# Pooled attention and top-1 experts in one kernel: another order for the first attention unit and for the expert loop

## The chip, the cores and the metric

The kernel runs on one core of one Trainium2 chip. The metric is device time in microseconds (us), the median of a few executions. TensorE (PE in the profile; PEld is its weight load), VectorE (DVE), ScalarE (ACT), GpSimd (POOL) and SyncE (SP, which here issues nearly all DMAs) run side by side and meet only at semaphores. Each engine takes its own instructions in the order in which they are written.

## The reference

```python
# attention: 8 batches, 8 heads, 576 tokens, 64 per head; keys and values are means over 8 tokens (72 of them)
k_p = k.reshape(B, H, Sp, 8, D).mean(axis=3); v_p = v.reshape(B, H, Sp, 8, D).mean(axis=3)
scores = (1 / sqrt(D)) * q @ k_p.T ; attn = softmax(scores) ; x = attn @ v_p      # -> 4608 rows of 512
# experts: 8, each 512 -> 1024 -> 512, one for each row
expert_idx = argmax(x @ w_gate) ; gate_w = softmax(x @ w_gate)[expert_idx]
y[row] = gate_w * (relu(x[row] @ w1[e]) @ w2[e])          # e = expert_idx[row]
```

All arrays are float32. Products in the experts are made of three float16 products each (high by high, high by low, low by high part), those of the scores in float32.

## The kernel before

**Attention.** The 4608 rows are 36 units of 128 rows. Two units with the same batch are a group; a group's queries are turned by TensorE (`g_qt`, L450, copied out by ACT at L453), and its scores are made in four steps of two heads each: `g_s` (the product, L473), `g_min` (DVE, L483), `g_exp` (ACT, L490). Then for each unit: `u_pt` turns the exponentials (L497) and ACT copies them to float16 (L499), `u_lo` makes the low part (DVE, L505), `u_pv` multiplies by the pooled values (L531), `u_nrm` divides (DVE, L563 to L574) and leaves the row block in a ring of 12 slots, `XR`. Later `route` finds the expert of each row, and POOL scatters the rows into one region for each expert in DRAM (`xs`).

For every batch the keys and values are pooled, three additions each. Batch 0 is pooled on DVE in two parts (`pool_now`, L322 to L324), batch 1 on POOL in five pieces of 128 pooled rows (`pool_short`, L306 to L308), later batches on POOL in whole tensors (`pool`, L313 to L316). `k_pe`/`k_act` turn the pooled keys and copy them into the block-diagonal right side `BD` of the score product (`half(b, s)`); `v_pe`/`v_act`/`v_dve`, `u_pe` and `u_dve` (with `masked`, L423) prepare the pooled values `VB`. Where each of these stands in the unit loop is a list of hooks (`put(unit, position, function)`); the positions of a unit are, in order, "q", "pe", "act", "dve", the product `u_pv`, "pe2", "sp", `u_nrm`, "act2", "dve2".

Group 0 and the first step of group 1 are written out ahead of the unit loop (L728 to L771): 36 dummy products, pooling of the keys, the queries' turns, the turns of the pooled keys one 64-column half at a time (L738, L739), their two copies on ACT (L741), then the four score steps with the value work between them.

**Experts.** A first block of 256 rows of expert 0 is multiplied during the last units. The rest are blocks of up to 256 rows in a loop, 21 passes in this run, with tables (`tabs`) that say for each block its row, its expert's weight set, whether a weight set has to be split (`en`), whether a block has more than 128 rows and which expert is to be loaded (`en3`). Weights arrive as float32 in two staging areas (`ST`: st1/st2 and, once the attention has finished, XR and pall) and are split into float16 high (ACT, L105) and low parts (DVE, L107) by `part` in the first block of an expert, for the next expert. A block is: 96 products `up` (L922 to L924), `relu_hi` (ACT, L981) and `relu_lo` (DVE, L985), `arrive` (DVE, L865: the turned x of the next block), `part`, 48 or 24 products `finish` (L991), `take` (ACT, L1170), `give` (POOL, L1173 to L1175: an indirect DMA to the output).

In a pass t the order on the queues is: SP reads its table entries; ACT and DVE run `split_x` (L853, L854: float16 parts of the x of block t+2, which lies in `xg`); SP issues `load_x(t + 3)` into `xg` (L1129); then the block; then SP issues `trans` (L861, a DMA transpose of what `split_x` made), the four weight loads of expert 2 in pass 0 (`If(t < 1)`, L1231, an `If` that every engine evaluates), and up to four weight loads of 1 MB for each staging area (L91, under the `If` at L1235). Where such an `If` isn't taken, SP waits in the other branch until the semaphores of those loads are where they would have been.

## Time and profile before

| | us |
|---|---|
| median of three runs (lowest to highest) | 660.05 (656.13 to 660.56) |
| the profiled execution, as timed | 661.64 |
| its span, first to last instruction | 659.8 |
| PE busy | 588.9 |
| DVE, ACT, POOL busy | 331.9, 286.0, 282.9 |
| mean granted clock of TensorE over the span | 0.961 |

The profile is of one execution. Its page gives busy times by engine, and its views answer for a stretch: a table of busy time by window, a timeline of one engine's instructions with what ended the idle time before each ("[1.78 <-ACT bd L981]" is 1.78 us of idle, ended by the instruction that wrote bd at L981), a list of waits, and the chain of waits that ended last. Instructions of one kind in a row are merged into one line with a count. The name of a buffer is that of its tile: bd holds the relu parts and the parts of x in the expert loop, kv0 the turned x, qt and kv the second weight set.

### The profile page before, as it was taken

The page shows a single profiled execution, that of the slowest core. Times are in us where ns is not written, and L with a number is a line of the kernel's source. Part 1 is how long each engine was busy: PE and PEld are TensorE (multiplying, and loading weights), DVE is VectorE, ACT ScalarE, POOL GpSimd, SP SyncE. Part 2 cuts the span into 40 slices and gives each one's busy share as a digit, 9 for nine tenths or more (in the row PEclk, how much of TensorE's full clock was granted, in tenths as well). Part 3 has the DMA queues.
Part 4 walks back from the last instruction along what each step waited for, and adds up shares of the span by engine and source line. Part 5 has one row for each costly group of instructions (what it writes and reads, how often), then busy time and mean ns, then how long its engine had stood idle before and what let it go on. Part 6 is the DMA issues. An engine that isn't in the chain of part 4 may idle for free. (4 is left out here: it accounts for less than half of the span.)

```text
span 659.8 us, 16297 instructions
## 1 busy us (share of the span) xinstructions
PE 588.9 (89%) x4634; PEld 429.8 (65%) x4635; DVE 331.9 (50%) x680; ACT 286.0 (43%) x631; POOL 282.9 (43%) x543
## 2 busy tenths in 40 slices
PE   6787897898878958997899799999999999999995
PEld 4676796887767544763576566675776666677663
DVE  5578985798896518202576176222362182221212
ACT  2565776777672126212565166123452181222212
POOL 5896589798695631222044242213132123212213
PEclk9998988998898979999899999999999999999998
DMA  9974778976749574953298387543232233312200
GB/s 257 307 233 124 219 221 243 225 238 184 241 98 312 179 175 141 374 163 81 64 308 303 73 269 235 184 116 100 45 90 66 71 80 83 80 48 64 64 16 29
DMA packets 104394, 105.59 MB, mean 160 GB/s; under 512 B 62502, under 2 KB 72742, under 8 KB 104360
## 3 DMA queue, kind: packets, MB, share of 16 engines
q1 hardware_dynamic: 97720, 85.46, 46.4%
q0 software_dynamic: 6640, 19.71, 8.1%
q8 instruction: 18, 0.29, 0.2%
q14 instruction: 16, 0.13, 0.1%
HBM read 71.77 MB, written 22.06 MB: 142 GB/s over the span
## 5 line engine op out<-in xcount | busy, mean ns | idle before, releaser
L991 PEld LDWEIGHTS <-bd 128*128 128x128 f16 x936 | 91.1, 98 | 114.0 <-ACT bd L981 6.7
L854 DVE TENSOR_TENSOR bd<-vb,bd 128x1024 f16<-128x1024 f32 x21 | 25.7, 1225 | 171.3 <-ACT bd L981 158.4
L1174 POOL TENSOR_TENSOR spacer<-ql,iG 1x1 f32<-1x1 f32 x44 | 21.2, 483 | 206.0 <-ACT ql L1170 205.1
L490 ACT ACTIVATE pall<-ps,nmx 128x72 f32<-128x72 f32 x288 | 68.8, 326 | 29.4 <-DVE nmx L483 28.6
L985 DVE SCALAR_TENSOR_TENSOR bd<-pp,bd 128x512 f16<-128x512 f32 x44 | 30.3, 690 | 75.9 <-ACT bd L981 65.6
L981 ACT ACTIVATE bd<-pp 128x512 f16<-128x512 f32 x44 | 26.2, 598 | 95.8 <-PE pp L924 64.9
L1175 POOL DMA_INDIRECT out_dram<-ql,iG x44 | 49.9, 1133 | 22.5 <-issue 21.9
L991 PE MATMUL po<-w,bd 128*128 128x512 f16 x264 | 58.8, 379 | 0.0
L991 PE MATMUL po<-kv,bd 128*128 128x512 f16 x264 | 58.8, 379 | 0.0
L473 PE MATMUL ps<-bd,qT 128*128 128x144 f32 x256 | 51.0, 329 | 5.6 <-ACT pall L490 2.1
L922 PE MATMUL ps<-kv,w 128*128 128x256 f16 (+1 forms) x176 | 44.5, 266 | 11.2 <-DMA kv<-bd 9.0
L991 PE MATMUL pq<-kv,bd 128*128 128x512 f16 x216 | 49.8, 389 | 3.6 <-ACT bd L981 3.6
L922 PE MATMUL ps<-kv,qt 128*128 128x256 f16 (+1 forms) x176 | 46.4, 268 | 6.2 <-issue 5.3
L531 PE MATMUL po<-vb,ph 128*128 128x146 f16 (+2 forms) x384 | 34.2, 237 | 19.3 <-DVE l L572 8.2
L924 PE MATMUL ps<-kv,qt 128*128 128x256 f16 (+1 forms) x176 | 46.2, 268 | 2.2 <-DVE bd L854 1.5
L853 ACT ACTIVATE bd<-vb 128x1024 f16<-128x1024 f32 x21 | 22.2, 1058 | 57.5 <-DMA kv<-bd 27.6
L923 PE MATMUL ps<-kv,qt 128*128 128x256 f16 (+1 forms) x176 | 46.5, 270 | 0.0
L922 PEld LDWEIGHTS <-w 128*128 128x128 f16 x352 | 34.9, 99 | 16.9 <-issue 9.8
L924 PE MATMUL ps<-kv,w 128*128 128x256 f16 (+1 forms) x176 | 44.6, 267 | 1.3 <-DVE w L107 1.3
L473 PEld LDWEIGHTS ps<-bd,qT 128*128 128x128 f32 x256 | 40.5, 217 | 7.7 <-ACT pall L490 4.8
L991 PE MATMUL pq<-w,bd 128*128 128x512 f16 x192 | 43.2, 379 | 2.0 <-ACT bd L981 1.8
L924 PE MATMUL pp<-kv,qt 128*128 128x256 f16 (+1 forms) x176 | 44.7, 263 | 0.0
(234 smaller groups left out, 1394.7 us busy)
## 6 DMA issues: line engine op xcount, KB each, us to landing
st<-in_moe_w_dram SPq DMA_DIRECT2D x20, 1024.0 KB, 9.7
XR<-in_moe_w_dram SPq DMA_DIRECT2D x9, 1024.0 KB, 7.3
vb<-x_by_expert SPq DMA_DIRECT2D x17, 514.0 KB, 3.8
kv<-in_k_dram SPq DMA_DIRECT2D x7, 1024.0 KB
kv<-in_v_dram SPq DMA_DIRECT2D x7, 1024.0 KB
qt<-in_q_dram SPq DMA_DIRECT2D x6, 1024.0 KB
pall<-in_moe_w_dram SPq DMA_DIRECT2D x3, 1024.0 KB, 9.8
qt<-in_q_dram SPq DMA_DIRECT2D x4, 512.0 KB
```

The lines of the kernel that those rows point to most:

```text
L473: nc.tensor.matmul(ps[:, x * 2 * KP:(x + 1) * 2 * KP], t[:, h, :], BD[b % 3][:, :, h, :], start=True, stop=True)
L490: nc.scalar.activation(p[:, h * KP:(h + 1) * KP], ps[:, x * KP:(x + 1) * KP], AF.Exp, bias=nmx[:, x:x + 1], scale=-1.0)
L531: nc.tensor.matmul(po[:, half, cols], a[:, c * 128:(c + 1) * 128], VB[b % 3][:, y, c, sl, 0:CW], start=st, stop=False, skip_group_check=True)
L853: nc.scalar.activation(h[:, :, 0], x, AF.Copy)
L854: nc.vector.tensor_tensor(h[:, :, 1], x, h[:, :, 0], op=OP.subtract)
L922: nc.tensor.matmul(dst, wh, xT[:, d, 0:n], start=(d == 0), stop=False)
L923: nc.tensor.matmul(dst, wh, xT[:, DC + d, 0:n], start=False, stop=False)
L924: nc.tensor.matmul(dst, wl, xT[:, d, 0:n], start=False, stop=(d == DC - 1))
L981: nc.scalar.activation(hT[0][:, 2 * k:2 * k + 2, :].rearrange("p f t -> p (f t)"), pH[k], AF.Relu)
L985: V.scalar_tensor_tensor(l, pH[k], 0.0, h, op0=OP.max, op1=OP.subtract)
L991: nc.tensor.matmul(y, hT[x][:, f, 128 * j:128 * j + 128], W2[s][z][:, f, :], start=(half == x == z == f == 0), stop=(half == z == 1 and f ...
L1175: st = nc.gpsimd.indirect_dma_start(out=out, out_offset=bass.IndirectOffsetOnAxis(ap=iG[:, j:j + 1], axis=0), in_=ys[j], in_offset=None, b ...
```

## The change

It does the following.

- 80 dummy products instead of 36 at the start, and 26 more (`keep_warm`) at four places of the first unit's steps.
- The pooled keys of batch 0 are written twice side by side by the last addition, so that one turn of 128 columns makes both halves; they lie in the ring's slots 10 and 11. Three of the turns stand ahead of the first turn of the queries. One copy into `BD` stays on ACT, the other goes to DVE, behind the first part of the values' pooling.
- In the opening the low part of the values (`v_dve`) stands earlier, the second half of group 0's queries later, and `u_pt` and `u_lo` of unit 0 ahead of the first score step of group 1. `k_pe`/`k_act` of batch 1 go from "pe"/"act" to "act2" of unit 0, `v_pe`/`v_act` from "pe"/"act" to "pe2"/"act2" of unit 1.
- `pool_short` works in three slices (2, 2 and 1 pieces) instead of five.
- The staging areas are single tiles, and an expert's weights are loaded by two DMAs of 2 MB (`wwhole`) instead of four of 1 MB.
- In the expert loop `split_x` goes from the head of the pass into the block, behind `arrive` and ahead of `part`; `load_x(t + 3)` goes behind `trans`; SP reads two more entries at the head; the loads of the staging areas follow in the order 0, 1; the `If(t < 1)` is gone, and two more DVE instructions in `table` put expert 2 into the entries of pass 0.

```diff
-WARM = 36
+WARM = 80
...
+    def wwhole(e, stage):
+        for src, dst in zip((w1d, w2d), WHOLE[stage]):
+            src = src[e:e + 1] if isinstance(e, int) else src[ds(e, 1)]
+            nc.sync.dma_start(dst, src.rearrange("e p c f -> p (e c) f"))
...
     def pool_short(src, dst):
-        for c in range(5):
+        for c in (slice(0, 2), slice(2, 4), slice(4, 5)):
...
+        if len(dst.shape) == 4:
+            n = c.stop - c.start
+            nc.vector.tensor_tensor(dst[:, c], p2[:, c, None, 0:D].to_broadcast([128, n, 2, D]),
+                                    p2[:, c, None, D:].to_broadcast([128, n, 2, D]), op=OP.add)
...
-    src, kp = pooled("kp", 0)
-    pool_now(src, kp, 0)
-    pool_now(src, kp, 1)
-    g_qt(0, 0)
-    g_qt(0, 1)
-    pm = psA.tile([128, 1024], F32, name="pp")
-    for c in (4, 2, 3, 0, 1):
-        n = 128 if c < 4 else 64
-        nc.tensor.transpose(pm[0:64, c * 128:c * 128 + n], kp[0:n, c], ident[0:n, 0:n])
-        nc.tensor.matmul(pm[64:128, c * 128:c * 128 + n], kp[0:n, c], ident[0:n, 0:n], start=True, stop=True)
-    for s in range(2):
-        nc.scalar.activation(half(0, s), pm[64 * s:64 * s + 64, 0:H * KP], AF.Copy, scale=-SC)
+    kp = both[:, 10 * XW:10 * XW + 10 * D].rearrange("p (c t d) -> p c t d", c=5, t=2)
+    pool_now(kv[0], kp, 0)
+    pool_now(kv[0], kp, 1)
     src, vp = pooled("vp", 0)
     pool_now(src, vp, 0)
+    pm = psA.tile([128, 1024], F32, name="pp")
...
+    turned((4, 2, 3))
+    g_qt(0, 0)
+    turned((0, 1))
+    nc.scalar.activation(half(0, 0), pm[0:64, 0:H * KP], AF.Copy, scale=-SC)
+    nc.vector.tensor_scalar(half(0, 1), pm[64:128, 0:H * KP], -SC, None, op0=OP.mult)
+    g_qt(0, 1)
+    pool_now(src, vp, 1)
+    keep_warm(8)
     now(0, 0)
-    pool_now(src, vp, 1)
     g_s(0, 1)
     v_pe(0)
     v_act(0)
     g_min(0, 1)
+    v_dve(0)
+    keep_warm(6)
     g_exp(0, 1)
...
-    u_dve(0)
+    u_dve(0, True)
     drain(0)
+    g_qt(1, 0)
+    keep_warm(6)
+    u_pt(0)
+    g_qt(1, 1)
     load_kv(1, vf)
...
-    g_qt(1, 0)
-    g_qt(1, 1)
+    u_lo(0)
     now(1, 0)
...
-    prep(1, (0, ""), (1, ""), (2, ""))
+    put(0, "act2", k_pe, 1)
+    put(0, "act2", k_act, 1)
+    put(1, "pe2", v_pe, 1)
+    put(1, "act2", v_act, 1)
...
         arrive()
+        split_x()
         part(s, en)
...
+        more = [entry(5, t + x, [ENG.SP], 0, 1) for x in (2, 3)]
         take_ids()
         move_ids()
-        split_x()
         keep_ids()
-        with tc.If(entry(5, t + 3, [ENG.SP], 0, 1) > 0):
-            load_x(t + 3)
         nc.gpsimd.drain()
...
-        with tc.If(entry(5, t + 2, [ENG.SP], 0, 1) > 0):
+        with tc.If(more[0] > 0):
             trans()
+        with tc.If(more[1] > 0):
+            load_x(t + 3)
         give(1)
-        with tc.If(t < 1):
-            for j in range(4):
-                wload(2, (2 * j, 2 * j + 2), 1)
-        for x in (1, 0):
+        for x in (0, 1):
             with tc.If(en3[x] > 0):
-                for j in range(4):
-                    wload(en3[x], (2 * j, 2 * j + 2), 1 - x)
+                wwhole(en3[x], 1 - x)
```

## Rows read from the trace of the kernel before

**Rows 1.** Table by window: length, busy (count) of PE, PEld, DVE, ACT, POOL, PEclk, DMA share, GB/s

```profile
264.00:380.00 116.00, 102.97 (x780) 68.95 (x781) 44.15 (x52) 41.91 (x57) 30.33 (x78) 0.96 0.61 194
380.00:660.00 280.00, 270.31 (x1982) 180.81 (x1979) 99.63 (x118) 96.04 (x132) 68.85 (x187) 0.99 0.34 97
```

**Rows 2.** Timeline of PE, opening: start us, us, line, op, count, [idle <-releaser]

```profile
1.67 4.02 PE L729 MATMUL po<-ones 128*128 128x128 f16 x36 [1.67 <-DVE ones L123]
8.78 1.97 PE L450 MATMUL pq<-ident,qt 128*128 128x128 f32 x8 [3.09 <-DMA qt<-in_q_dram]
...
39.48 0.73 PE L473 MATMUL ps<-bd,qT 128*128 128x144 f32 x4
```

**Rows 3.** Timeline of DVE, opening

```profile
10.83 0.96 DVE L322 TENSOR_TENSOR st<-kv 128x768 f32<-128x768 f32 x1 [1.69 <-DMA kv<-in_v_dram]
...
12.41 0.36 DVE L324 TENSOR_TENSOR vp<-st 128x192 f32<-128x192 f32 x1
...
25.33 0.54 DVE L379 SCALAR_TENSOR_TENSOR vc<-vp,vc 128x320 f16<-128x320 f32 x1
```

**Rows 4.** Timeline of DVE, the same instruction one batch later

```profile
43.80 2.40 DVE L379 SCALAR_TENSOR_TENSOR vc<-vp,vc 128x320 f16<-128x320 f32 x1
```

**Rows 5.** Timeline of ACT, opening

```profile
15.31 1.30 ACT L741 ACTIVATE bd<-pp 64x576 f32<-64x576 f32 x2 [3.93 <-PE pp L739]
...
25.45 0.96 ACT L490 ACTIVATE pall<-ps,nmx 128x72 f32<-128x72 f32 x4 [1.42 <-DVE nmx L483]
```

**Rows 6.** Timeline of POOL: batch 1 (first, two middle, last pieces), a later tensor

```profile
18.51 1.16 POOL L306 TENSOR_TENSOR st<-kv 128x256 f32<-128x256 f32 x1 [7.89 <-DMA kv<-in_k_dram]
...
22.24 0.73 POOL L306 TENSOR_TENSOR st<-kv 128x256 f32<-128x256 f32 x1
...
23.86 0.73 POOL L306 TENSOR_TENSOR st<-kv 128x256 f32<-128x256 f32 x1
...
37.25 0.32 POOL L308 TENSOR_TENSOR vp<-st 128x64 f32<-128x64 f32 x1
...
42.95 2.90 POOL L313 TENSOR_TENSOR st<-kv 128x1280 f32<-128x1280 f32 x1
```

**Rows 7.** Timeline of PE, expert loop: the two late starts of finish

```profile
297.26 3.04 PE L991 MATMUL pq<-w,bd 128*128 128x512 f16 x12 [1.78 <-ACT bd L981]
...
375.76 7.10 PE L991 MATMUL pq<-kv,bd 128*128 128x512 f16 x24 [3.60 <-ACT bd L981]
```

**Rows 8.** Chain that ended last, undisturbed halves of finish: start us, us, what

```profile
445.37 5.18 PE po L991 x24
455.91 5.18 PE po L991 x24
```

**Rows 9.** Timeline of ACT in the same two passes

```profile
295.66 1.06 ACT L853 ACTIVATE bd<-vb 128x1024 f16<-128x1024 f32 x1 [9.77 <-DMA kv<-bd]
...
374.16 1.06 ACT L853 ACTIVATE bd<-vb 128x1024 f16<-128x1024 f32 x1 [12.25 <-DMA kv<-bd]
```

**Rows 10.** Timeline of SP: its only DMAs from 274 to 290 us

```profile
274.39 0.37 SPq L91 DMA_DIRECT2D st<-in_moe_w_dram  x1
288.98 0.39 SPq L1129 DMA_DIRECT2D vb<-x_by_expert  x1
```

**Rows 11.** Waits on SP's queue, 264 to 400 us: total us, times, longest

```profile
SPq L1235 <- SPq L1235: 17.3, 7, 4.0
```

**Rows 12.** PE's sequencer at L1231: count, ns least/median/most, first and last start

```profile
L1231 PEldq COMPARE_BRANCH  x22: 84/225/230, 261.7 to 650.9; - x22
```

**Rows 13.** Timeline of PE, expert loop: first products of a pass after a short block

```profile
328.83 0.28 PE L924 MATMUL ps<-kv,w 128*128 128x256 f16 x1 [0.63 <-DVE w L107]
...
461.92 0.27 PE L922 MATMUL ps<-kv,qt 128*128 128x256 f16 x1 [0.82 <-issue]
```

**Rows 14.** Page, groups: count, busy us, mean ns, idle before and what ended it

```profile
L854 DVE TENSOR_TENSOR bd<-vb,bd 128x1024 f16<-128x1024 f32 x21 | 25.7, 1225 | 171.3 <-ACT bd L981 158.4
```

**Rows 15.** Timeline of DVE in the pass before 328.83

```profile
325.29 6.90 DVE L107 SCALAR_TENSOR_TENSOR w<-XR,w 128x1024 f16<-128x1024 f32 x6
```

More of the change, by code (lines that the diff above doesn't have):

```diff
@@ L72 @@
     walloc(consts, 0)
-    st1 = [consts.tile([128, 2, F], F32, name=f"st1_{i}") for i in range(2)]
-    st2 = [consts.tile([128, 4, Dm], F32, name=f"st2_{i}") for i in range(2)]
+    sa1 = consts.tile([128, DC, F], F32, name="st1")
+    sa2 = consts.tile([128, FC, Dm], F32, name="st2")
+    st1 = [sa1[:, 2 * i:2 * i + 2, :] for i in range(2)]
+    st2 = [sa2[:, 4 * i:4 * i + 4, :] for i in range(2)]
     w1d = w1.rearrange("e (c p) f -> e p c f", p=128)
@@ L219 @@
     pbig = st1[0].rearrange("p c x -> p (c x)")
-    pall = loads.tile([128, 4, 640], F32, name="pall")
-    pbuf = [pall[:, i, :] for i in range(4)]
-    XR = loads.tile([128, 12, XW], F32, name="XR")
-    xr = XR.rearrange("p u x -> p (u x)")
-    ST.append(([xr[:, o:o + 2048].rearrange("p (c f) -> p c f", c=2) for o in (0, 2048)],
-               [x.rearrange("p (c f) -> p c f", c=4)
-                for x in (xr[:, 4096:6144], pall.rearrange("p i x -> p (i x)")[:, 0:2048])]))
+    both = loads.tile([128, 12 * XW + 4 * 640], F32, name="both")
+    XR = both[:, 0:12 * XW].rearrange("p (u x) -> p u x", x=XW)
+    pbuf = [both[:, 12 * XW + 640 * i:12 * XW + 640 * i + 640] for i in range(4)]
+    sb1 = both[:, 0:DC * F].rearrange("p (c f) -> p c f", c=DC)
+    sb2 = both[:, DC * F:DC * F + FC * Dm].rearrange("p (c f) -> p c f", c=FC)
+    ST.append(([sb1[:, 2 * i:2 * i + 2, :] for i in range(2)], [sb2[:, 4 * i:4 * i + 4, :] for i in range(2)]))
+    WHOLE.append((sb1, sb2))
     kf = k.rearrange("b h (s j) d -> b (h s) (j d)", j=POOL)
@@ L414, in low @@
                         moves.append((VB[b % 3][r0:r1, :, c, s, 0:D + E], vc[r0:r1, :, c, :]))
-        first = [lambda: v_dve(b), cross, gather, high, low]
+        first = [cross, gather, high, low] if early else [lambda: v_dve(b), cross, gather, high, low]
         if b < 2:
@@ L729, with keep_warm, turned @@
         nc.tensor.matmul(warm[:, 0, 0:128], ones, ones, start=True, stop=True)
[L730 to L741 removed]
+    def keep_warm(n):
+        for _ in range(n):
+            nc.tensor.matmul(warm[:, 1, 0:128], ones, ones, start=True, stop=True)
+    kp = both[:, 10 * XW:10 * XW + 10 * D].rearrange("p (c t d) -> p c t d", c=5, t=2)
+    pool_now(kv[0], kp, 0)
+    pool_now(kv[0], kp, 1)
     src, vp = pooled("vp", 0)
     pool_now(src, vp, 0)
+    pm = psA.tile([128, 1024], F32, name="pp")
+    def turned(cs):
+        for c in cs:
+            n = 128 if c < 4 else 64
+            nc.tensor.transpose(pm[:, c * 128:c * 128 + n], kp[0:n, c].rearrange("p t d -> p (t d)"), ident[0:n, 0:n])
+    turned((4, 2, 3))
[6 more added lines that the diff above has]
+    keep_warm(8)
     now(0, 0)
[L745 removed]
     g_s(0, 1)
@@ L938 @@
         flush(1)
-        u_pt(i)
+        if i:
+            u_pt(i)
         if A:
@@ L948 @@
         run(i, "pe")
-        u_lo(i)
+        if i:
+            u_lo(i)
         fill()
@@ L1162 @@
             wsplit(1, j)
-        for j in range(4):
-            wload(3, (2 * j, 2 * j + 2))
+        wwhole(2, 1)
+        wwhole(3, 0)
     T = nc.values_load(tab[0:1, 0:1], min_val=1, max_val=TMAX)
```

12 lines of the change are left out of this document (9 added, 3 removed).

## The prediction

> **What bounds the kernel now.** I read the table by window first, for PE's share of each stage: 102.97 of 116 us are PE's from 264 to 380 and 270.31 of 280 us after that [rows 1]. From 264 us on, only what stalls PE costs time: some 13 us in the first stretch, some 10 in the second. Then the timelines, with what ended each idle stretch. In the opening PE is cold or idle and the path runs over landings, DVE, ACT and POOL; in the loop, two halves of `finish` start late for one named reason.
>
> The sum is made against the profiled execution, 661.64 us, which is 1.59 above the median of 660.05; at the end I take that off. 1% is 6.6 us, about what a measurement of this kernel can tell from no change.
>
> **The opening.** Before, both halves of `BD` come out of ACT at 15.31 + 1.30 = 16.61, after ACT waited 3.93 us for the half-column turns [rows 5]. PE had done 36 dummies by 1.67 + 4.02 = 5.69, sat 3.09 us until the queries landed, and turned them first, eight in 1.97 us [rows 2]. After: 80 dummies at 4.02/36 = 0.112 end at 10.6; that is later than 8.78, but the nine turns left (three, four, two) at 1.97/8 = 0.246 end at 12.8. DVE's copy stands behind the first part of the values' pooling, which waits 1.69 us for its landing and ends at 12.41 + 0.36 = 12.77 [rows 3]. A copy is half of 1.30, 0.65, so `BD` is ready at about 13.5: 3.1 earlier. All 44 added dummies lie in that wait, as do the 26 later ones in waits for DVE and ACT; without that cover they would cost 70 x 0.112 = 7.8. The keys' doubled write on DVE lies in the 1.69 us wait. That a clock raised by the dummies shortens the turns further changes nothing, since DVE's copy cannot start before 12.77.
>
> The last exponentials of unit 0 end at 25.45 + 0.96 = 26.41 now [rows 5]. Putting the second part of the values behind the first on DVE takes its three additions out of the score steps, and the second half of the queries' turns leaves their gap on PE; I estimate another 2.7, so 5.8 at most.
>
> That isn't what reaches the rest. PE's product at 39.48 [rows 2] stands behind the values of batch 1, which POOL ends at 37.25 + 0.32 = 37.57, and the next tensors follow on POOL without a gap. POOL begins at 18.51, when the keys land, in both kernels [rows 6]. A piece takes 23.86 - 22.24 = 1.62, a whole tensor (five pieces in one slice) 42.95 - 37.57 = 5.38. With a fixed part a per slice and b per piece, a + b = 1.62 and a + 5b = 5.38: b = 0.94, a = 0.68. Three slices take 2.04 + 4.70 = 6.74, two tensors 13.5 instead of 16.2: 2.7 less. The ten pieces took 37.57 - 18.51 = 19.06, so 2.86 went to slower single ops; if that shrinks with the number of slices (six for ten), 1.1 more goes, 3.8 in all. I take the middle, **-3.3**, to the end of the opening. Bounds: 0 (lost in later waits) and -5.8.
>
> What is moved here: `k_act` of batch 1 now stands behind the unit's other ACT work, so group 2's scores have less spare; `v_pe` stands after more of unit 1's PE work, which is where the gain of POOL can vanish. `u_pt` and `u_lo` of unit 0 ahead of group 1's scores only change places.
>
> A row speaks against larger slices on POOL: the same DVE instruction takes 0.54 us at 25.33 [rows 3] and 2.40 at 43.80 [rows 4], while POOL's 2.90 us addition runs from 42.95 [rows 6]. The Trainium skill, "SBUF — State Buffer", section "Who interferes with whom", says that a DVE instruction with two SBUF inputs contends with a GpSimd instruction that reads SBUF, and that whoever comes first holds the shared ports for its whole instruction; the trace agrees in kind (0.54 against 2.40). By that rule a two-piece slice (about 0.73 + 0.54 = 1.27 for its first op) would hold DVE up to 0.54 longer than a one-piece op, on average 0.27, on four ops +1.1, and the sum would be 652.4. I leave it out, since fewer ops also mean fewer holds.
>
> **The expert loop.** (a) The half at 297.26 starts 1.78 late, the one at 375.76 starts 3.60 late and runs at 7.10 instead of 5.18 [rows 7, 8]: the same 24 products, so a lower clock after the idle time costs 1.92 more. Both wait for ACT's `relu_hi`. ACT had `split_x` at the head of its queue, and that waited 9.77 and 12.25 us for x [rows 9]. x was late since SP issued nothing between the weight load at 274.39 and `load_x` at 288.98 [rows 10]: it sat in the branch at L1235 that waits for those loads, 17.3 us in seven waits up to 400 us [rows 11]. After the change `relu_hi` stands ahead of `split_x`, and `trans` and `load_x` ahead of the weights' loads. The stall goes: **-1.8** and **-(3.60 + 1.92) = -5.5**. Bounds 0 (another wait) and -7.3. Next late would be the x of the block after; its load and turning take 295.66 - 288.98 = 6.7 us [rows 9, 10], and a short pass lasts 455.91 - 445.37 = 10.5 [rows 8], so 3.8 are spare in the worst place.
>
> (b) `If(t < 1)` on every engine: PE's sequencer spends 0.225 us in it, 22 times [rows 12], 5.0 in all; but PE runs on queued products in most passes. It shows where a pass begins with idle time that nothing releases, 0.82 at 461.92 [rows 13], four places. I take 4 x 0.225 = **-0.9**, bounds 0 and -5.0. The two entries that SP reads at the head lie on SP alone, which has time.
>
> (c) On DVE `split_x`'s low part, 1.225 us [rows 14], was done in idle time; now it is between the relus and the weight splits. In most passes DVE has slack (99.63 of 280 us busy) [rows 1]. Where the next block begins a new expert after a short pass, PE already waits for the last split: at 328.83 for DVE's L107, six of which (6.90) had started at 325.29 [rows 13, 15]. Two such places: 2 x 1.225 = **+2.4**, bounds 0 and +6 x 1.225 = 7.4 (each of the experts loaded).
>
> (d) Two more instructions in `table`: nearest by size are small DVE ops, none above 0.36 [rows 3]; one chain, once: **+0.3**, bounds 0 and 0.7. One DMA of 2 MB for two of 1 MB, expert 2 loaded before the loop or by the table: needed a whole expert later, 0; if it weren't hidden, 4 MB at 194 GB/s [rows 1] are 21.6 us, the worst case behind the last rival.
>
> **Sum.** -3.3 - 1.8 - 5.5 - 0.9 + 2.4 + 0.3 = -8.8: 661.64 - 8.8 = 652.8 for an execution like the profiled one, 651.3 at the median.
>
> **The rivals.** First, the opening's gain is lost between 62 and 216 us: for it, the many short waits of that stage and POOL's tensors back to back; against it, that POOL itself ends earlier. Then -5.5 of the loop is left: 654.6. Second, the loop's stalls come back under another name (splits or weights late), the opening stays: -3.3 - 0.9 + 2.7 = -1.5, 658.6. For it: the 0.63 on L107 [rows 13]. Third, slower: x's load or turning queues behind a 2 MB transfer. It decides from 3.8 us of delay on; then three of the six loading passes stall by 5.5 each, with the two old stalls gone: -3.3 - 0.9 + 2.7 - 7.3 + 16.5 = +7.7, 667.8. For it, 21.6 us of transfer beside a 6.7 us chain; against it, that SP's branch still waits for the loads in the passes between.
>
> **How the numbers follow.** The forecast has 0.60 (its own range 645.5 to 655), the first rival 0.15, the second 0.14, the third 0.11. From 645 (opening -5.8, no late splits) to 659 (second rival) leaves out the third and a little of the forecast. Faster by over 1% (below 653.4): 0.55 of the forecast and 0.06 of the first rival, 0.61; within 1%: the rest of these and the second rival, 0.28; slower: the third, 0.11.
>
> **What would show it.** Right: `BD`'s second copy ends near 13.5, the last exponentials near 20.6, POOL's batch 1 near 34.3, the product of 39.48 near 36.2; no idle time before L991 that ACT's L981 ends; no compare-branch of an `If(t < 1)`; L107 1.2 us later at the boundary after 328.83. Wrong: POOL's batch 1 still near 37.6; new idle time before L991 or L922 ended by L853, L854, L107 or a landing of x; a lower granted clock in the loop.

## The result

The changed kernel takes 650.44 us (median of four runs, 646.10 to 650.64), the kernel before 659.42 in the runs beside it (656.13 to 660.56): ratio 0.9858, 95% interval 0.9823 to 0.9894. 651.3 was predicted. The profiled execution of the changed kernel was timed at 650.54 and spans 648.1 us, that of the kernel before 661.64 and 659.8.

The total was right to 0.1%, but not every term behind it, and the two parts of the change did not gain what they were said to. Here the difference of the two profiled spans, 11.7 us, is cut at places that both traces have: the starts of the products of the attention's units and of the 22 `finish` runs (numbered 0 to 21 in order of time; 0 is the block ahead of the loop). The `If`'s 0.9 is spread over its four places; finish 5 to 6 took the same in both.

| stretch | predicted | difference in the traces |
|---|---|---|
| start to unit 7's product (72.04, now 69.07) | -3.3 | -3.0 |
| from there to finish 0 (221.50, now 215.35) | +0.3 | -3.2 |
| finish 0 to 2 | -0.2 | -0.5 |
| finish 2 to 3 (the late start at 297.26) | -1.8 | -1.9 |
| finish 3 to 4 (first short block) | 0 | -4.9 |
| finish 4 to 5 (next block begins an expert) | +1.2 | +3.0 |
| finish 6 to 8 (the late start at 375.76) | -5.7 | -5.6 |
| finish 8 to 15 | -0.2 | -0.2 |
| finish 15 to 16 (next block begins an expert) | +1.0 | +3.9 |
| finish 16 to the end | 0 | +0.7 |

First the table by window of the changed kernel, for the two stretches that [rows 1] shows of before (columns as there).

```profile
264.00:380.00 116.00, 110.20 (x833) 73.39 (x831) 54.32 (x61) 50.80 (x66) 29.96 (x78) 0.99 0.68 212
380.00:648.00 268.00, 257.29 (x1871) 171.15 (x1868) 88.58 (x106) 87.64 (x120) 61.07 (x176) 0.98 0.32 91
```

PE now works 110.20 of 116 us where it was 102.97 [rows 1]; in the rest it idles 10.7 us where it was 9.7. So the loop gained in the first stretch and lost a little in the second. The lists of waits of PE from finish 1 to the end say what changed. First the kernel before (waiting instruction, what ended the wait: total us, times, longest):

```profile
PE pq L991 <- ACT bd L981: 5.4, 2, 3.6
PE ps L922 <- issue: 5.3, 3, 3.7
PE ps L922 <- DVE kv L107: 2.1, 1, 2.1
PE ps L924 <- DVE bd L854: 1.5, 1, 1.5
PE ps L924 <- DVE w L107: 1.3, 2, 0.6
...
PE ps L924 <- DVE qt L107: 0.7, 2, 0.5
```

Then the changed kernel, where L1027 is `finish`, L956 to L958 `up`, L1017 `relu_hi`, L116 the low part of a weight split, L888 that of x:

```profile
PE ps L956 <- issue: 3.0, 2, 2.4
PE ps L956 <- DVE kv L116: 2.7, 1, 2.7
PE ps L958 <- DVE w L116: 2.6, 4, 0.7
PE ps L958 <- DVE qt L116: 1.6, 4, 0.5
```

The two waits of `finish` for `relu_hi` (5.4 us) are gone without a trace. The waits for the low part of a weight split have grown from 1.3 and 0.7 to 2.6 and 1.6 us at the two places that were forecast, and from 2.1 to 2.7 at a third, between finish 1 and 2. That is what was forecast, in kind. What they cost is more than the waits, as the granted clock shows. This is the table by window, from the end of a short pass's `finish` to the start of the next, at the two places: the first two lines are of the kernel before, the two in the second fence of the changed one.

```profile
326.81:339.26 12.45, 10.99 (x96) 9.19 (x97) 10.01 (x10) 7.92 (x11) 6.09 (x9) 1.00 0.91 288
535.58:548.27 12.69, 11.14 (x97) 9.14 (x97) 10.23 (x10) 8.09 (x11) 6.20 (x9) 1.00 0.23 42
```

```profile
313.27:328.75 15.48, 12.77 (x97) 9.95 (x97) 10.37 (x10) 8.37 (x11) 5.93 (x12) 0.89 0.78 234
519.30:535.91 16.61, 14.28 (x98) 10.39 (x97) 10.43 (x11) 8.43 (x11) 6.13 (x13) 0.79 0.28 66
```

The same 96 products keep PE busy 12.77 and 14.28 us instead of 10.99 and 11.14, since TensorE was granted 0.89 and 0.79 of full speed: part of each stretch was at the low one of its two levels. It fell while PE was fed in drops, three products for each weight split. Of +3.0 at the first place, 1.8 is PE being busy longer; of +3.9 at the second, 3.1.

In the opening, the timelines of the changed kernel (idle time and what ended it in brackets). PE:

```profile
15.00 1.25 PE L487 MATMUL ps<-bd,qT 128*128 128x144 f32 x8 [2.98 <-DVE bd L764]
...
28.28 1.33 PE L487 MATMUL ps<-bd,qT 128*128 128x144 f32 x4 [4.56 <-ACT both L504]
...
40.06 0.76 PE L487 MATMUL ps<-bd,qT 128*128 128x144 f32 x4
```

DVE, the copy of the keys and the two masked operations on the values:

```profile
14.19 0.76 DVE L764 TENSOR_SCALAR bd<-pp 64x576 f32<-64x576 f32 x1
...
22.02 4.12 DVE L437 TENSOR_TENSOR vb<-vc,mk 128x1080 f16<-128x1080 f16 x2
```

ACT, the last exponentials of unit 0, and POOL, the last piece of batch 1's values:

```profile
20.97 0.96 ACT L504 ACTIVATE both<-ps,nmx 128x72 f32<-128x72 f32 x4 [0.38 <-DVE nmx L497]
```

```profile
34.50 0.32 POOL L317 TENSOR_TENSOR vp<-st 128x64 f32<-128x64 f32 x1
```

DVE's copy of the keys ends at 14.95 (13.5 forecast; the values landed 1.4 later than in the trace of before [rows 3]), the last exponentials of unit 0 at 21.93 (20.6 forecast, 26.41 before [rows 5]), and POOL's values of batch 1 at 34.82 (34.3 forecast, 37.57 before [rows 6]), all within 1.5 us of the forecast. The fourth sign failed: the product that stood at 39.48 [rows 2], the score step behind unit 1's product, stands at 40.06 (36.2 forecast). Unit 0's product was 3.3 us earlier (30.25 for 33.55), but the turns of batch 1's keys now stand behind it, and PE ran slowly from 28.28 on, after a wait of 4.56 us (four score products took 1.33 us there and 0.76 at 40.06), so unit 1's product started at 37.99 where it was 38.28. (In two more executions of the changed kernel it started at 33.94 and 34.55.)

The lead comes at unit 4, whose product started at 57.38 and now at 54.66. First the kernel before, DVE, POOL and PE:

```profile
48.67 2.77 DVE L406 TENSOR_TENSOR vc<-u,vc 128x40 f16<-128x40 f32 x1
...
48.49 2.89 POOL L313 TENSOR_TENSOR st<-kv 128x1280 f32<-128x1280 f32 x1
...
57.38 0.95 PE L531 MATMUL po<-vb,ph 128*128 128x146 f16 x12 [2.83 <-DVE l L572]
```

Then the changed kernel:

```profile
47.55 1.16 DVE L420 TENSOR_TENSOR vc<-u,vc 128x40 f16<-128x40 f32 x1
...
45.77 2.89 POOL L322 TENSOR_TENSOR st<-kv 128x1280 f32<-128x1280 f32 x1
...
54.66 1.43 PE L545 MATMUL po<-vb,ph 128*128 128x146 f16 x12 [2.83 <-DVE l L586]
```

In both, a small DVE operation ends 0.05 to 0.06 us after POOL's addition beside it (51.44 and 51.38, now 48.71 and 48.66), DVE works on without a gap, and unit 4's product waits for the end of that work. POOL's tensors are 2.7 us earlier, and so is the product: POOL does set the pace here, a few units later than the prediction had it. Whether that is what sets the kernel's time is another question, to which the experiments come.

### The profile page after: what moved, and what is told of

It reads as the page before. It is cut to its first block, busy times and chain, and to the rows that moved or that the text cites. A ratio compares the mean times of both kernels' runs of the same rounds, so it can differ in the third digit from the quotient of the medians.

```text
span 648.1 us, 15925 instructions
## 1 busy us (share of the span) xinstructions
PE 585.6 (90%) x4694; PEld 430.1 (66%) x4695; DVE 329.9 (51%) x683; ACT 286.2 (44%) x630; POOL 275.6 (43%) x531
## 5 line engine op out<-in xcount | busy, mean ns | idle before, releaser
L1027 PEld LDWEIGHTS <-bd 128*128 128x128 f16 x936 | 91.3, 98 | 105.7 <-ACT bd L1017 1.0
L1212 POOL TENSOR_TENSOR spacer<-ql,iG 1x1 f32<-1x1 f32 x44 | 23.8, 540 | 220.7 <-ACT ql L1208 219.7
L1021 DVE SCALAR_TENSOR_TENSOR bd<-ps,bd 128x512 f16<-128x512 f32 x44 | 30.1, 689 | 152.2 <-ACT bd L1017 152.2
L504 ACT ACTIVATE both<-ps,nmx 128x72 f32<-128x72 f32 x288 | 68.7, 326 | 29.5 <-DVE nmx L497 28.8
L1017 ACT ACTIVATE bd<-pp 128x512 f16<-128x512 f32 x44 | 26.2, 597 | 108.9 <-PE pp L958 78.8
L1017 ACT ACTIVATE bd<-ps 128x512 f16<-128x512 f32 x44 | 26.1, 597 | 77.3 <-PE L956 67.9
L487 PE MATMUL ps<-bd,qT 128*128 128x144 f32 x256 | 49.6, 322 | 11.2 <-ACT both L504 5.5
L1027 PE MATMUL po<-kv,bd 128*128 128x512 f16 x264 | 58.8, 379 | 0.0
L1027 PE MATMUL po<-w,bd 128*128 128x512 f16 x264 | 58.8, 379 | 0.0
L1213 POOL DMA_INDIRECT out_dram<-ql,iG x44 | 43.8, 995 | 21.8 <-issue 20.2
L956 PE MATMUL ps<-kv,w 128*128 128x256 f16 (+1 forms) x176 | 44.8, 268 | 8.5 <-DMA kv<-bd 5.6
L956 PE MATMUL ps<-kv,qt 128*128 128x256 f16 (+1 forms) x176 | 46.1, 270 | 4.5 <-issue 3.0
L1027 PE MATMUL pq<-kv,bd 128*128 128x512 f16 x216 | 48.1, 379 | 0.0
L487 PEld LDWEIGHTS ps<-bd,qT 128*128 128x128 f32 x256 | 39.1, 210 | 13.0 <-ACT both L504 8.4
L958 PE MATMUL ps<-kv,qt 128*128 128x256 f16 (+1 forms) x176 | 46.2, 270 | 1.6 <-DVE qt L116 1.6
L545 PE MATMUL po<-vb,ph 128*128 128x146 f16 (+2 forms) x384 | 34.3, 237 | 14.8 <-DVE l L586 6.6
L958 PE MATMUL ps<-kv,w 128*128 128x256 f16 (+1 forms) x176 | 44.9, 268 | 2.6 <-DVE w L116 2.6
L957 PE MATMUL ps<-kv,w 128*128 128x256 f16 (+1 forms) x176 | 44.9, 268 | 0.0
L956 PE MATMUL pp<-kv,qt 128*128 128x256 f16 (+1 forms) x176 | 44.7, 263 | 0.0
L957 PE MATMUL pp<-kv,qt 128*128 128x256 f16 (+1 forms) x176 | 44.7, 263 | 0.0
```

Source lines behind the costliest of these rows:

```text
L487: nc.tensor.matmul(ps[:, x * 2 * KP:(x + 1) * 2 * KP], t[:, h, :], BD[b % 3][:, :, h, :], start=True, stop=True)
L504: nc.scalar.activation(p[:, h * KP:(h + 1) * KP], ps[:, x * KP:(x + 1) * KP], AF.Exp, bias=nmx[:, x:x + 1], scale=-1.0)
L545: nc.tensor.matmul(po[:, half, cols], a[:, c * 128:(c + 1) * 128], VB[b % 3][:, y, c, sl, 0:CW], start=st, stop=False, skip_group_check=True)
L956: nc.tensor.matmul(dst, wh, xT[:, d, 0:n], start=(d == 0), stop=False)
L957: nc.tensor.matmul(dst, wh, xT[:, DC + d, 0:n], start=False, stop=False)
L958: nc.tensor.matmul(dst, wl, xT[:, d, 0:n], start=False, stop=(d == DC - 1))
```

## The experiments

Comparisons were made on several chips, each with the kernel before beside it: its median was 667.9, 667.2, 660.9 and 661.7 us there, so only ratios are compared across groups. One profiled execution of a kernel differs from the next by some us; a profile shows the mechanism, the ratio the price.

**The opening alone, and the loop alone.** The changed kernel with the loop, its tables and its weight loads of before (`e1_open`):

```diff
         arrive()
-        split_x()
         part(s, en)
...
+        split_x()
         keep_ids()
+        with tc.If(entry(5, t + 3, [ENG.SP], 0, 1) > 0):
+            load_x(t + 3)
...
-                wwhole(en3[x], 1 - x)
+                for j in range(4):
+                    wload(en3[x], (2 * j, 2 * j + 2), 1 - x)
```

> The new opening with the expert loop, its tables and its weight loads of before. Theory: the opening is worth about 3 us in the attention (the product of unit 1 and those after it start 3.0 earlier than in the kernel before) and the further 3.2 us that the changed kernel shows by its first finish (221.50 became 215.35) hang on DVE's instruction of 1.72 us at 198.15 in the trace of before, which met POOL there: 653.8, with the late halves of finish (1.8 and 3.6) still there. Rival A: that meeting is a matter of the opening's phase and comes back anywhere: 3 us only, 656.9. Rival B: the opening's gain is swallowed between 62 and 216 us: 660.

And the changed kernel with the opening of before (`e2_loop`): 36 dummies, half-column turns, both copies on ACT, five slices on POOL, batch 1 at its old places.

```diff
-    put(0, "act2", k_pe, 1)
-    put(0, "act2", k_act, 1)
-    put(1, "pe2", v_pe, 1)
-    put(1, "act2", v_act, 1)
...
+    prep(1, (0, ""), (1, ""), (2, ""))
```

> The new expert loop, tables and weight loads with the opening of before. Theory: two late halves of finish go (-7.3), the stall of the first short block shrinks (-4.9 in the trace of the changed kernel), and the two new-expert passes after a short block cost +3.0 and +3.9, other places -0.9: about -6.2, 653.5. Rival: the two parts of the change depend on each other (the loop's gain needs the earlier end of the attention): 656 or more. By both theories DVE's instruction of 1.72 us at 198 stays, as the attention is that of before.

Measured: the opening alone 0.9835 (0.9769 to 0.9902), the loop alone 0.9959 (0.9923 to 0.9995), on the same chip. Both parts gain, and the opening more than the loop: of 667.9 us, 11.0 (6.5 to 15.4) and 2.7 (0.3 to 5.1), where the prediction had 3.3 for the one and 5.5 for the other. Neither of these lies in its interval; each part was wrong by itself, in opposite directions. Nor do the parts add: the versions with both on this chip (`e3_behind`, `e4_head`, below) measured 0.9833 and 0.9836, no better than the opening alone. In the traces the two differ by 3.2 us at the start of finish 1 (248.79 and 251.94), which is about the opening's gain as forecast, and less than the 8 us between the medians; and the opening-only kernel still has its late halves of `finish` (1.03 and 2.35 us of idle before them). The loop-only kernel has lost them, but its first short block took 24.53 us from finish 3 to finish 4 (24.20 before, 19.29 in the changed kernel's first trace), and its new-expert passes 19.03 and 21.71 (17.80 and 18.03 before; 17.72 and 20.23 in the opening-only kernel, so the second of them can be long with the old loop too).

So the 4.9 us of the first short block do not belong to the loop's change alone. From finish 3 to finish 4 the changed kernel took 19.29, 21.35 and 21.09 in three executions, and the six other versions that have SP's new order in the loop and the new opening with its dummy products 19.37 to 21.80. The four that lack one of these took 23.2 to 24.5: the kernel before 24.20, the opening alone 23.24, the loop alone 24.53, and the version without the added dummies (`e6_cold`) 23.23. That holds on each of the chips on which both kinds were traced. What differs is seen in windows over the short block, from the end of finish 3 to the end of finish 4: the changed kernel, then the loop alone.

```profile
299.16:313.27 14.11, 11.68 (x121) 7.83 (x120) 4.49 (x7) 5.63 (x8) 2.55 (x10) 1.00 0.12 38
```

```profile
308.70:328.05 19.35, 14.10 (x120) 10.25 (x121) 4.69 (x7) 5.83 (x8) 2.55 (x10) 0.82 0.09 28
```

In both PE first waits for nothing that the profile shows (2.36 and 3.02 us, "issue"), in the second it stops once more (2.19), and then runs on a lowered clock (0.82). The kernel before had much the same (3.71 us, then 1.46 ended by DVE's low part of x, clock 0.81). In these traces it took the loop and the opening together to shorten the stretch; why is open.

**Which of two edits ended the late halves of `finish`?** The changed kernel with `split_x` back at the head of the pass, but SP's new order kept (`e4_head`):

```diff
         move_ids()
+        split_x()
         keep_ids()
...
         arrive()
-        split_x()
         part(s, en)
```

> The changed kernel with split_x back at the head of the pass, as before, but with SP's new order (turning and x ahead of the weights' loads). Theory: SP's order alone made x late, so the late halves of finish (1.8 and 3.6) stay away and the weight splits are no longer held up: 643.5. Rival: the place on ACT's queue ahead of the relus is the cause whatever SP does: relu_hi waits again for x at the two passes, +7.3 less 6.9 for the splits, 650.8.

Measured 0.9836 (0.9767 to 0.9906). Its timelines at the two passes, of PE and then of ACT:

```profile
295.37 1.96 PE L1027 MATMUL pq<-w,bd 128*128 128x512 f16 x8 [1.63 <-ACT bd L1017]
...
369.61 2.44 PE L1027 MATMUL pq<-kv,bd 128*128 128x512 f16 x10 [1.79 <-ACT bd L1017]
```

```profile
293.77 1.06 ACT L887 ACTIVATE bd<-vb 128x1024 f16<-128x1024 f32 x1 [9.63 <-DMA vb<-x_by_expert]
...
368.01 1.06 ACT L887 ACTIVATE bd<-vb 128x1024 f16<-128x1024 f32 x1 [10.77 <-DMA vb<-x_by_expert]
```

ACT again waits 9.63 and 10.77 us for x with the relus queued behind, where it waited 9.77 and 12.25 [rows 9], and `finish` starts 1.63 and 1.79 us late where it was 1.78 and 3.60 [rows 7]. My expectation fell: SP's new order alone gets x there little earlier. In this version `load_x` was issued at 289.85, behind a turning that took SP 10.81 us (from 276.55). So SP's order is not enough; the place on ACT's queue, relus first, is needed. Whether that place alone would do, with SP's old order, was not run. Nor is it shown that SP's order takes anything off the second stall (1.79 for 3.60), which was 2.35 in `e1_open` with the old order. In return the new-expert passes are back at 17.78 and 18.74, and the kernel's ratio is about that of the changed one on other chips.

**The low part of x ahead of the weight splits.** Behind all of `part` (`e3_behind`):

```diff
         arrive()
-        split_x()
         part(s, en)
+        split_x()
```

> The changed kernel with split_x moved behind part (arrive, part, split_x). Theory: the low part of split_x (1.22 us on DVE) ahead of the weight splits is what starves PE at the two passes after a short block, and the clock that falls there costs more than the stall: 3.0 and 3.9 us come back, 643.5. Rival A: these passes wait for the weights' landing (one DMA of 2 MB), whatever stands ahead on DVE: 650.4. Rival B: x is now split 9 us later, its turning comes late and the next block waits for it: 652 or more, with idle time before the first product of a pass that DVE's arrive ends.

Measured 0.9833 (0.9757 to 0.9908): no better than the changed kernel, and yet the theory holds at its place. The new-expert passes take 17.99 and 18.90 us instead of 20.82 and 21.95. But finish 6 to 8, 37.78 us in the changed kernel, takes 41.54. The timelines of SP and DVE there:

```profile
346.83 2.09 SPq L895 DMA_TRANSPOSE kv<-bd  x1
...
354.26 1.20 SPq L87 DMA_DIRECT2D st<-in_moe_w_dram  x2
360.01 8.43 SPq L895 DMA_TRANSPOSE kv<-bd  x1
```

```profile
352.78 0.69 DVE L899 COPY kv<-kv 128x2048 f16<-128x2048 f16 x1 [2.79 <-DMA kv<-bd]
...
370.62 0.69 DVE L899 COPY kv<-kv 128x2048 f16<-128x2048 f16 x1 [2.74 <-DMA kv<-bd]
373.40 3.50 DVE L116 SCALAR_TENSOR_TENSOR w<-both,w 128x1024 f16<-128x1024 f32 x3 [2.08 <-ACT w L114]
```

A turning of x takes SP 2.09 us to issue when the queue is free and 8.43 when it stands behind the 4 MB of weights issued at 354.26. Two passes are 1.8 and 1.9 us longer. In the first, the turning of 346.83 is late only because x was split late: `arrive` waits 2.79 us for it, and PE 2.23 before the next products. In the second, SP was held for 8.43 us; `arrive` waits 2.74, ACT's next weight split waits 5.20 for SP's branch at L1271, which stood behind the turning, and DVE's low part follows it. The second is the third rival of the prediction, x's turning behind the transfers, in a small form. In the changed kernel such a hold is there too but hidden:

```profile
272.95 10.05 SPq L895 DMA_TRANSPOSE kv<-bd  x1
```

SP spent 10.05 us there, behind four weight loads (8 MB), and finish 2 to 3 still took 20.84 us, as every full pass without a stall. What an early `split_x` buys is this room.

So a place between the two: w1's four splits first, which the next block wants at once, then x, then w2's (`e9_mid`).

```diff
-    def part(s, en):
+    def part(s, en, js):
...
         arrive()
+        part(s, en, range(4))
         split_x()
-        part(s, en)
+        part(s, en, range(4, 8))
```

> The changed kernel with split_x between the fourth and the fifth weight split (w1's four parts first, then x, then w2's). Theory: only w1's splits are wanted at once by the next block, so the two passes after a short block win back most of 3.0 and 3.9 us, and x is late by 4.6 us only, not 9.1 as with split_x behind all of part, so the turning stays ahead of the 2 MB transfers more often: 2 to 6 us under the changed kernel. Rival: any delay of the turning puts it behind the weights' transfers and the passes that follow lose 1.8 and 1.9 us again as with split_x behind part: within 1 us of that kernel, and of the changed kernel.

And the changed kernel beside it (`a1_after`), unchanged:

> The changed kernel itself, beside the others of this group. Ratio to the kernel before 0.986 as in the first comparison. Theory: passes after a short block that begin a new expert take 20.8 and 22.0 us from finish to finish (4 to 5, 15 to 16), as in its first trace. The 5 us by which its first short block was faster than in the kernel before (24.2 to 19.3 us from finish 3 to finish 4) are a matter of the execution and not of the change: 20 to 24 here. Rival: they belong to the change and come again: 19.3.

Measured: 649.37 us and 0.9738 (0.9691 to 0.9785) against 657.53 and 0.9866 (0.9822 to 0.9909) for the changed kernel on the same chip. The intervals do not touch: this version beats the changed kernel beside it. (`e3_behind` was measured on another chip, and its interval touches this one's.) Its timeline of DVE in the short pass before finish 16, and the window after that pass:

```profile
521.80 0.68 DVE L899 COPY kv<-kv 128x2048 f16<-128x2048 f16 x1
522.40 4.62 DVE L116 SCALAR_TENSOR_TENSOR qt<-st,qt 128x1024 f16<-128x1024 f32 x4
526.94 1.22 DVE L888 TENSOR_TENSOR bd<-vb,bd 128x1024 f16<-128x1024 f32 x1
528.08 4.62 DVE L116 SCALAR_TENSOR_TENSOR kv<-st,kv 128x1024 f16<-128x1024 f32 x4
```

```profile
523.45:536.44 12.99, 11.16 (x96) 9.14 (x97) 10.54 (x11) 8.36 (x11) 5.31 (x9) 1.00 0.35 80
```

The first four splits follow `arrive` directly, the clock stays at 1.00, and the pass takes 18.90 us (21.73 beside it); finish 4 to 5 takes 17.96 (19.07 beside it), finish 6 to 7 takes 17.72 (16.94). From the start of finish 1 to the end of the last one the loop lasts 391.4 us against 397.7. Of those 6.3, 3.9 are the two passes, less 0.8 at finish 6 to 7; 1.6 come from finish 1 to 2, where PE idled 1.21 us instead of 2.84, and 1.5 from the first short block (1.35 of idle for 2.87), which may be luck. The traces' attention differed the other way by 4.6 us, so the 8.2 us between the medians are not accounted for one by one.

**What in the opening gains?** POOL's five slices back (`e7_five`):

```diff
-        for c in (slice(0, 2), slice(2, 4), slice(4, 5)):
+        for c in range(5):
```

> The changed kernel with POOL's pooling of batch 1 in five slices, as before. Theory of the prediction: larger slices are worth 2.7 to 3.8 us, as the values of batch 1 set the pace: POOL ends them near 37.5 to 38.5 instead of 34.8 and the attention is 3 us later: 3 us slower than the changed kernel. Rival: shorter POOL instructions hold DVE less (the masked values took 4.12 us and not 2.59 beside the larger slices, and PE idled 4.56 us behind them), so what POOL loses DVE gains: within 1 us.

Measured 0.9845 (0.9805 to 0.9886), the changed kernel beside it 0.9866: no difference. Its timelines of POOL and PE:

```profile
37.18 0.32 POOL L317 TENSOR_TENSOR vp<-st 128x64 f32<-128x64 f32 x1
```

```profile
34.88 0.95 PE L545 MATMUL po<-vb,ph 128*128 128x146 f16 x12
...
37.56 0.30 PE L373 MATMUL pq<-ident,vp 128*64 128x128 f32 x1 [1.09 <-POOL vp L317]
```

POOL takes 37.50 - 19.29 = 18.2 us for the ten pieces and, in the changed kernel on the same chip, 15.5 for the six: 2.7 less, the very figure of the prediction's sum. But unit 1's product starts at 34.88 without waiting, and only the turn of the values behind it waits, 1.09 us (0.80 in the changed kernel). Further on PE does follow POOL. The turn of batch 2's values, in the changed kernel and then here:

```profile
48.35 0.44 PE L371 MATMUL pq<-ident,vp 128*128 128x128 f32 x2 [0.72 <-POOL vp L325]
```

```profile
49.57 0.44 PE L371 MATMUL pq<-ident,vp 128*128 128x128 f32 x2 [0.70 <-POOL vp L325]
```

POOL began 1.5 us earlier here (19.29 for 20.78, when the keys landed), so it ends batch 1 only 1.23 later, and unit 4's product starts 1.21 later (52.03 for 50.82), unit 7's 3.4 later (68.22 for 64.85), finish 1 1.7 later. So POOL's gain reaches the units, but it is not seen in the time of the kernel.

The five slices and also batch 1's work back at its old places (`e11_hooks`), beside the changed kernel once more (`a2_after`):

```diff
-        for c in (slice(0, 2), slice(2, 4), slice(4, 5)):
+        for c in range(5):
...
-    put(0, "act2", k_pe, 1)
-    put(0, "act2", k_act, 1)
-    put(1, "pe2", v_pe, 1)
-    put(1, "act2", v_act, 1)
...
+    prep(1, (0, ""), (1, ""), (2, ""))
```

> The changed kernel with POOL's pooling of batch 1 in five slices, as before, and the work on batch 1's keys and values back at its old places (k_pe, k_act at pe and act of unit 0, v_pe, v_act at pe and act of unit 1). Theory: it is this move, not the slices, that took POOL off PE's path, since the values are asked for behind unit 1's product and no longer ahead of it. With both undone unit 1's product waits for POOL again (38 and not 34 to 35 us) and the kernel is 2 to 4 us slower than the changed one. Rival: the opening's gain comes from the order of group 0's steps alone, and where batch 1 is asked for is indifferent: unit 1 may start later but the attention ends at the same time, within 1 us of the changed kernel.

> The changed kernel itself, once more, as what the other run of this group is compared with: ratio to the kernel before 0.986; unit 1's product near 34 to 38 us, first short block (finish 3 to 4) anywhere between 19.3 and 23.2 us.

Measured 0.9833 (0.9789 to 0.9877) and 0.9835 (0.9794 to 0.9876): the same. In its timeline of PE:

```profile
35.82 0.47 PE L371 MATMUL pq<-ident,vp 128*128 128x128 f32 x1 [2.90 <-POOL vp L317]
37.44 0.42 PE L373 MATMUL pq<-ident,vp 128*64 128x128 f32 x1 [1.14 <-POOL vp L317]
```

Now PE does wait for POOL at unit 1, 2.90 and 1.14 us, and unit 1's product starts at 38.44 instead of 34.55. In the two profiled executions the lead is still 3.2 us at finish 1 (245.59 and 242.39), and the loops differ the other way (393.96 and 398.04 us: 1.7 and 1.3 of it are the two new-expert passes, in which the clock stayed at 1.00 here and fell to 0.89 there, and 1.3 is finish 1 to 2). The medians of six runs are 649.23 and 649.61. So the move of the hooks takes POOL off PE's path at unit 1, as the theory said, but 3 us in the attention did not show in the time of the kernel. Which of the opening's edits gives the 0.9835 of `e1_open` stays open; one more was taken out:

**The dummy products** (`e6_cold`), 36 and none of the 26:

```diff
-WARM = 80
+WARM = 36
...
-    keep_warm(8)
```

> The changed kernel with 36 dummy products at the start, as before, and none of the 26 later ones. Theory of the prediction: they lie in waits and the clock that they hold up is worth nothing, since PE waits for DVE's copy of the keys (14.95): same as the changed kernel, within 1 us. Rival: they keep the clock up through the first unit; without them its score products run at the low level (8 in 2.3 us and not 1.25) and the attention is 2 to 3 us later.

Measured 0.9891 (0.9856 to 0.9926), 660.02 us, the changed kernel beside it 0.9866 and 657.53. The intervals overlap; 2.5 us stay possible and are not shown. The windows of the first 34 us, first with 36 dummies, then the changed kernel beside it, with 106:

```profile
0.00:34.00 34.00, 23.77 (x131) 21.08 (x133) 20.91 (x55) 12.60 (x40) 24.02 (x60) 0.70 0.97 278
```

```profile
0.00:34.00 34.00, 23.86 (x221) 21.40 (x223) 21.36 (x56) 14.47 (x46) 21.79 (x56) 0.95 0.97 263
```

The clock is 0.70 with 36 and 0.95 with 106; the first eight score products took 2.29 us here and 1.46 in the changed kernel (2.29 in the kernel before, 1.25 in the changed kernel's first trace). Unit 1's product starts at 37.26 here and at 33.94 there. So the dummies do raise the clock. That they move the first units by 3.3 us is not shown by one pair, since with them unit 1's product started at 37.99 in the changed kernel's first trace; at finish 1 the two differ by 1.5 us.

**The `If` and the size of a DMA.** The `If(t < 1)` back, without the two instructions in `table` (`e8_if`):

```diff
+        with tc.If(t < 1):
+            wwhole(2, 1)
         for x in (0, 1):
```

> The changed kernel with the If(t < 1), which every engine evaluates in every pass, back in its place around expert 2's load, and without the two instructions in table. Prediction: the If costs 0.2 us at each of four places where PE waits at a pass's start, and the two instructions 0.3 us: +0.9 - 0.3 = +0.6 against the changed kernel, not to be told from nothing (ratio 0.986 to 0.989); the idle times before the first product at these places grow from 0.65 to 0.85 by 0.2. Rival: it costs PE 0.225 us in each of 22 passes, 5 us: ratio 0.994.

Measured 0.9792 (0.9735 to 0.9849): not slower than the changed kernel, on the same chip at another time 0.9835. Where passes begin after a short block the timeline of PE shows, first with the `If`, then without it (`a2_after`):

```profile
523.06 0.27 PE L956 MATMUL ps<-kv,qt 128*128 128x256 f16 x1 [1.01 <-ACT qt L114]
```

```profile
521.46 0.27 PE L956 MATMUL ps<-kv,qt 128*128 128x256 f16 x1 [0.71 <-ACT qt L114]
```

0.30 us at this place, and the stretches of finish 6 to 7 and 11 to 12 are longer by 0.27 and 0.30. At four places that would be some 1.2 us (an estimate), about the 0.9 of the sum, and too little to be seen in the time. That it would cost all 22 passes (5 us) is excluded.

Four loads of 1 MB for two of 2 MB (`e5_mb`):

```diff
-                wwhole(en3[x], 1 - x)
+                for j in range(4):
+                    wload(en3[x], (2 * j, 2 * j + 2), 1 - x)
```

> The changed kernel with an expert's weights loaded in the loop by four DMAs of 1 MB instead of two of 2 MB. Theory of the prediction: the size is worth nothing, as the weights are needed an expert later: same as the changed kernel within 1 us, ratio 0.986. Rival: 2 MB in one DMA is what holds the turning of x on SP's queue for up to 10 us in the changed kernel; in smaller ones it is held less, and the passes in which the weights are loaded are 1 to 3 us shorter together. A third: SP issues four more DMAs and its loads of x come later: 1 to 3 us longer.

Measured 0.9883 (0.9820 to 0.9947), 653.1 us: not told apart from the changed kernel. Its profiled execution took 2789.32 us and says nothing of the others, so whether a turning is held less behind smaller transfers stays open.

## Why the prediction came out right, point by point

**The late halves of `finish`, -1.8 and -5.5.** Right: -1.9 and -5.6, with the lowered clock after the idle time rightly counted as a part of the price [rows 7, 8]. In all the kernels with the new loop and the relus first, finish 2 to 3 took 20.84 us. The prediction let two edits end the stall, SP's order and the place behind the relus; `e4_head` shows that the first alone does not. The price was that of one execution: in `e1_open`, with the old loop, the same waits were 1.03 and 2.35 us and the stretches 1.2 and 3.3 longer than 20.84 and 37.78. That is one reason why the loop alone gained 2.7 us and not 5.5.

**The split of x ahead of the weight splits, +2.4.** The mechanism was right and the two places too (finish 1 to 2 is a third, +0.7), and the size was off: the term measured 3.0 + 3.9 in the first trace, 1.3 + 3.7 and 3.0 + 2.6 in two more (19.07 and 21.73, 20.79 and 20.61 us from finish to finish, against 17.80 and 18.03 before). The sum counted the delay, 1.225 twice, and PE's idle time in the two stretches did grow by 1.25 (2.71 for 1.46) and 0.78 (2.33 for 1.55). What it left out is that a PE fed in drops can lose its clock (0.89 and 0.79 where it had 1.00), 1.8 and 3.1 us. It is the same effect that the prediction had charged for the late halves of `finish` a paragraph earlier; a lower clock in the loop was one of its signs of being wrong. It does not come each time: the eight traces with x's split ahead of all weight splits have 16 such passes, and in six of them the clock stayed at 1.00. These took 19.0 to 19.1 and 19.4 us, 1.2 to 1.3 more than before, about the size of the sum; the ten in which it fell took 20.3 to 22.0. With x's split elsewhere it fell in one pass of ten (`e1_open`, 20.23 us). `e9_mid`, `e3_behind` and `e4_head` give most of the loss back, at 1.00.

**The opening, -3.3.** Its size was right in the first pair of traces (-3.0 by unit 7), and so was the step named as its cause, POOL's pace, though not at the place named: at the product of 39.48 nothing was gained, from unit 4 on the 2.7 us that POOL gained. At unit 1 the edit that the prediction listed as a mere move ("where the gain of POOL can vanish") is the one that frees PE of POOL (`e11_hooks`). But the step from there to the kernel's time failed: without the slices (`e7_five`), and without the slices and the moves (`e11_hooks`), unit 7's product is 3.4 and 5.5 us later and the time is the same, while the opening as a whole measured 11.0 us and not 3.3. What gives it is open.

**The ports of SBUF.** The prediction left out a possible price of larger slices, 1.1 us. Two masked operations on DVE took 4.12 us in the changed kernel's first trace beside POOL's slices, 3.00 and 2.73 in two more, and 2.72 with five slices; before it was 2.59. So the larger slices can hold DVE, and PE's wait that ends at 28.28 stands behind it (4.56 us; 3.31 and 2.80 in the two more, but 3.41 with five slices, so it has other causes too). The trace agrees in kind with "SBUF — State Buffer" in the Trainium skill, section "Who interferes with whom" (whoever comes first holds the shared ports for its whole instruction). The clearest case is in the kernel before, in the timelines of DVE and POOL:

```profile
198.15 1.72 DVE L665 TENSOR_SCALAR res<-res 128x6 f32<-128x6 f32 x1
```

```profile
197.71 2.13 POOL L114 TENSOR_TENSOR w<-kv,w 128x1024 f16<-128x1024 f32 x1
```

A DVE instruction on six columns, issued while POOL's addition ran, ends at 199.87, 0.03 us after POOL's (199.84). The units' last divisions stood behind it, and PE idled 2.15 us from 199.83 (the profile names a DMA as what ended that wait, so the link is argued). In the changed kernel's first trace PE has no such wait there, which is part of the 3.2 us that it gained between unit 7 and finish 0. The meeting is a matter of phase and no part of the change; six of the other traces with the new opening have an idle time of 1.87 to 2.60 us of PE at that place for other reasons, among them the changed kernel itself (2.02).

**The `If`, -0.9, and the table, +0.3.** Both as forecast where the trace can show them (0.27 to 0.30 at three places; PE's wait for the tables grew from 0.75 to 1.01, and was 0.74 in `e8_if`, without the two instructions), neither visible in the time.

**The first short block, 0.** Wrong for the pair of traces (-4.9), which made good what the weight splits cost beyond the forecast (6.9 for 2.4). The prediction put this stretch at nothing; yet all nine traces with SP's new order and the new opening with its dummies have 19.3 to 21.8 us there, and the four that lack one of them 23.2 to 24.5, so some of it belongs to the change, by a way that was not found. The -3.2 between unit 7 and finish 0, forecast at +0.3, was not named either. So it is luck that the total fell close: in this pair of traces errors of opposite sign cancel, and in the times the opening gained more than forecast, the loop less, and the two together less than their sum.

**The rivals.** The third (slower: x behind the weights' transfers) was real as a mechanism, 10.05 us of SP at 272.95, and decided nothing since the turning had more room than the 3.8 us that the prediction gave it: x of a block is wanted a whole pass later. `e3_behind` shows where the room ends: with x split 9.1 us later two passes lose 1.8 and 1.9. The first, the opening's gain lost on the way, is not borne out by this pair (3.0 us at unit 7, 6.2 at finish 0). The second, the loop's stalls back under another name, came true in part: late weight splits took back 6.9 of the 7.5 us that the late halves of `finish` had cost.

## What to carry to other kernels

Count what a stall can do to the clock, not its length alone: where PE was fed in drops by another engine and its clock fell, the price was 2.4 and 5 times the wait that was added (3.0 for 1.25 us, 3.9 for 0.78); where it did not fall, the wait alone. When work is to be put into another engine's queue, look for the gap in what the next consumer needs at once: half the splits before x and half behind it gave 0.9738 where x ahead of all gave 0.9866 beside it (and x behind all 0.9833 on another chip). Before a faster producer is counted as a gain, look for who waits for it after the change, not before. And measure the parts of a change by themselves: here the total was forecast well and neither part was.

## What the runs showed of the hardware

A DMA transpose of one block's x took SP 2.09 us to issue on a free queue, 8.43 behind 4 MB of weights and 10.05 behind 8 MB: the engine that issues is held, with all that it would issue next. A DVE operation on 40 columns, issued beside POOL's addition, took 2.77 us and ended 0.06 us after it. TensorE's first eight score products took 2.29 us behind 36 dummy products and 1.25 and 1.46 behind 88. Fed in drops, TensorE lost its full clock in ten of 16 like passes, and these took 1.2 to 2.6 us more than the six in which it kept it. Three executions of one program differed by 2.1 us in one place (the first short block, 19.29 to 21.35 us), where PE stops for 2.4 to 2.9 us with nothing that the profile shows to release it. The place of a long wait can also differ: in two traces of the changed kernel PE waited 1.0 us for the tables ahead of finish 0 and then 4.3 and 5.6 us for the first x behind it, in a third 8.5 us for the tables and nothing for x (the second and the third are of two chips).
